# Linear attention before a mixture of experts: scores in four 64x64 tiles, compact states, and their product ahead of the transpositions

## The chip, the core and the metric

The kernel runs on one core of a Trainium2 chip. The metric is the device time of one execution in microseconds, from the median of three runs.

## The reference

Three layers follow each other. The first, the only one that the change touches, is block-wise attention with a decay, over 4 batches, 8 heads, 768 positions and a head size of 64:

```python
for b in range(nb):
    intra = np.einsum('bhic,bhjc->bhij', qb, kb) * Dmask[None]
    intra = np.einsum('bhij,bhjd->bhid', intra, vb)
    inter = np.einsum('bhid,bhde->bhie', qb * lam_pow[None], kv_state)
    out[:, :, sl] = intra + inter
    kb_dec = kb * rev_pow[None]
    kv_state = lam_block[None, :, None, None] * kv_state + np.einsum('bhsd,bhse->bhde', kb_dec, vb)
```

So each block has scores of its own (`intra`) and reads a 64x64 state per head (`inter`), which it then renews. The second layer is a soft mixture of 8 experts with 32 slots over the 3072 tokens, the third a dense layer with a sigmoid-approximated GELU, out of `w_in` (512x2048) and `w_out` (2048x512).

## The kernel before, in words

All is fp32. The attention takes blocks of 128 positions in place of the reference's 64, which is the same sum. Its unit of work is a step: one batch, one half of the sequence (384 positions, three chunks of 128) and one pair of heads. There are 32 steps (`NSTEP`); four of them, the four pairs of heads, make a group, and groups alternate between the first and the second half of a batch. The two heads of a pair stand in partitions 0 to 63 and 64 to 127.

For a step s the functions are, with the lines of the profile:

- `do_q` and `do_T` (L250, L259, L261): ScalarE reorders q, TensorE transposes q and k against an identity, and ScalarE copies both out of their banks as qT (L269) and kT (L272).
- `do_SC` (L297, L300): the score products kT times qT, per chunk one matmul for each head, in rows 0 to 63 or 64 to 127 of the array; VectorE multiplies with the decay and writes AT. The two heads have a bank each, s0 and s1.
- `do_kd` (L285): k times its decay, on ScalarE. `do_qd` (L278): qT times the powers of lambda, on POOL.
- `do_ST` (L310, L319, L321): kd times v, a 64x64 product per head and chunk; VectorE adds it to the decayed state before. A state is a 128x128 tile with the two heads on its diagonal and zeros elsewhere, which POOL writes once (L517). The state of the last chunk of a first half is kept for the second half (`S_3`).
- `do_XS` (L336): the product of the states with qdT, per chunk one matmul over all 128 rows. It opens the bank x. In the first half of a sequence its first chunk has no state and is left out.
- `do_XA` (L344): AT times v is added in the same bank; ScalarE then copies the bank out as xT (L347).
- `do_XT` (L355, L356): xT is transposed back and stored as xn for the mixture of experts.

The eight banks are named and each is single, so a writer waits until the tile before in its bank has been read. The order on each engine is the order in which the loop (L531) calls these functions: an iteration i issues the scores of step i + 1, the transpositions of q and k of step i + 2, the transposition back of step i − 1, the state product of step i, the new states of step i + 1, kd of step i + 2 and AT times v of step i. Between them stand parts of the mixture of experts, spread over four iterations (`ph`): with `ph` 0 the logits of the group before and the slots of the one before that (L365, L437), with `ph` 1 the transposition of the logits (L374), with `ph` 2 a maximum (L408), with `ph` 3 the exponentials (L423, L429, L431).

In every second iteration from 2 to 20 a block of `w_in` or `w_out` is brought to its range by ScalarE, VectorE and POOL in `do_early` (L180, L189 to L195, L202); its transfer, `stage`, was issued on SP an iteration earlier. SP also issues the loads of q, k and v, three to five steps ahead, and those of the expert weights.

Of the kernel before, what the change touches and what calls it, by code (L numbers as in the profile page):

```python
# [8 lines left out]
F32 = mybir.dt.float32  # L9
# [3 lines left out]
ALU = mybir.AluOpType  # L13
# [4 lines left out]
def attention_moe_gelu_kernel(  # L18
# [14 lines left out]
    PE, ACT, DVE, POOL, SP = nc.tensor, nc.scalar, nc.vector, nc.gpsimd, nc.sync  # L33

    B, H, S, D = q.shape
    P = 128
    NHP = H // 2
    HS = 384
    R = HS // P
# [10 lines left out]
    NSTEP = NG * NHP  # L50
# [25 lines left out]
    attn = attn_cm.__enter__()  # L76
# [154 lines left out]
        by_turns(conversion(("early", c), o, POOL))  # L231


    S_a = [attn.tile([P, P], F32, tag=f"sa{i}", name=f"sa{i}", bufs=1) for i in range(4)]
    S_3 = [attn.tile([P, P], F32, tag=f"s3{i}", name=f"s3{i}", bufs=1) for i in range(NHP)]

    def state(s, c):

        b, hf, hp, g = step_of(s)
        if c == R:  # L240
            return S_3[hp]
        return S_a[2 * (s % 2) + (c - 1 if c < R else c - R - 1)]
# [46 lines left out]
    def do_SC(s):  # L289

        b, hf, hp, g = step_of(s)
        bs = [bank(f"s{h}", "bs") for h in range(2)]
        for c in range(R):
            cs = slice(c * P, (c + 1) * P)
            for h in range(2):
                hs = slice(h * D, (h + 1) * D)
                PE.matmul(bs[h][:, cs], kT[s][hs, cs], qT[s][hs, cs], start=True, stop=True)  # L297
        for h in range(2):
            t = attn.tile([P, R, P], F32, tag=f"AT{h}", name="AT")
            DVE.tensor_tensor(out=t, in0=bs[h][:, :HS].rearrange("m (c i) -> m c i", c=R),  # L300
                              in1=dec[:, 2 * hp + h, None, :].to_broadcast([P, R, P]), op=ALU.mult)
            AT[s, h] = t

    def do_ST(s):
        b, hf, hp, g = step_of(s)
        bst = bank("st", "bst")
        nchunk = [c for c in range(R) if hf * R + c < NHF * R - 1]
        for c in nchunk:
            for h in range(2):
                PE.matmul(bst[h * D:(h + 1) * D, c * D:(c + 1) * D], kd[s][:, c, h, :],  # L310
                          v_t[s][:, c, h, :], start=True, stop=True)
        for c in nchunk:
            cg = hf * R + c
            new = state(s, cg + 1)
            for h in range(2):
                r = slice(h * D, (h + 1) * D)
                src = bst[r, c * D:(c + 1) * D]
                if cg == 0:
                    DVE.tensor_copy(out=new[r, r], in_=src)  # L319
                else:  # L320
                    DVE.scalar_tensor_tensor(out=new[r, r], in0=state(s, cg)[r, r],  # L321
                                             scalar=qtab[r, hp, P - 1:P], in1=src,
                                             op0=ALU.mult, op1=ALU.add)

    bxs = {}

    def do_XS(s):

        b, hf, hp, g = step_of(s)
        bx = bxs[s] = bank("x", "bx")  # L330


        first = hf * R
        chunks = [c for c in range(R) if first + c > 0]
        for c in chunks:
            PE.matmul(bx[:, c * P:(c + 1) * P], state(s, first + c), qdT[s][:, c, :],  # L336
                      start=(c == chunks[0]), stop=False)

    def do_XA(s):

# [138 lines left out]
    with tc.manual_schedule():  # L479
# [27 lines left out]
        n = 1  # L507
# [5 lines left out]
        load_step(2, "k")  # L513
        load_step(2, "q")
        load_step(3, "q")
        for t in S_a + S_3:
            POOL.memset(t, 0.0)  # L517
        POOL.memset(ones, 1.0)

        def make_isum():  # L520
# [10 lines left out]
        for i in range(-2, NSTEP):  # L531
            g, ph = divmod(i, NHP)
            if i > -2:
                load_step(i + 5, "q")
            if i == 1:
                make_isum()

            if 0 <= i + 1 < NSTEP:
                do_SC(i + 1)
            if 0 < i + 2 < NHP:  # L540

                for h in range(2):
                    make_dec(2 * (i + 2) + h)

            if 0 <= i + 2 < NSTEP:
                do_T(i + 2)
                if i == -2:
                    warm_up(1)
            if 0 <= i - 1 < NSTEP:
                do_XT(i - 1)  # L550
            if 0 <= i + 3 < NSTEP:
                do_q(i + 3)
            if ph == 1 and 0 <= g - 1 < NG:
                tail_L(g - 1)
            if ph == 2 and 0 <= g - 1 < NG:
                tail_max(g - 1)
            if ph == 3 and 0 <= g - 1 < NG:
                tail_exp(g - 1)
            if i == NSTEP - 1:
                tail_logits_first(NG - 1)  # L560
            if 0 <= i < NSTEP:
                do_XS(i)

            if 0 <= i + 1 < NSTEP:
                do_ST(i + 1)
            if 0 <= i + 2 < NSTEP:
                do_kd(i + 2)
            if 0 <= i < NSTEP:
                do_XA(i)

            if ph == 0 and 0 <= g - 1 < NG:
                tail_logits(g - 1)
            if ph == 0 and 0 <= g - 2 < NG:
                tail_z(g - 2, "tk")
                tail_slot(g - 2)
                tail_acc(g - 2)
            if i == NSTEP - 4:
                load_pieces(i + 1)

            load_pieces(i)  # L580

            load_step(i + 5, "k")
            c, turn = divmod(i - 2, EVERY)
            if turn == 1 and 0 <= c + 1 < len(EARLY):
                load_early(c + 1)
            if i >= 0:
                load_step(i + 3, "v")
            if 0 <= i + 2 < NSTEP:
                do_qd(i + 2)
            if i == -2:  # L590
                load_step(2, "v")
                SP.dma_start(out=phi_sb, in_=phi.rearrange("(k p) s -> p k s", p=P))
            if turn == 0 and 0 <= c < len(EARLY):
                do_early(c)
            if ph == 3 and 0 <= g - 1 < NG and i < NSTEP - 1:
                tail_row(g - 1)
            if ph == 0 and 0 <= g - 2 < NG:
                tail_row_exp(g - 2)
            if i == NSTEP - 2:
                early_cm.__exit__(None, None, None)  # L600
                slotb_cm = tc.tile_pool(name="slotb", bufs=NPC_B, side="right", reuse_waits="tile")
                slotb = slotb_cm.__enter__()

                rooms = [piece_room(NPC + j) for j in reversed(range(NPC_B))]
                while rooms:
                    load_piece(rooms.pop())
            if i == NSTEP - 1:
                attn_cm.__exit__(None, None, None)
                slotc_cm = tc.tile_pool(name="slotc", bufs=NPC_C, side="left", reuse_waits="tile")
                slotc = slotc_cm.__enter__()  # L610
                for _ in range(NPC_C):
                    load_piece()
# [712 lines left out]
```

## Time and profile before

| | |
|---|---|
| Median of three runs | 488.8 us (488.13 to 491.09) |
| Profiled execution | 490.36 us |
| Its span, first to last instruction | 488.5 us |
| TensorE busy (PE) | 471.3 us |
| VectorE (DVE), ScalarE (ACT), POOL | 369.8, 302.6, 77.7 us |
| Attention loop, 6.59 to 147.94 us | 141.35 us; TensorE busy 136.29, VectorE 112.85, ScalarE 102.58 |

PEld is TensorE's weight load, which can run beside a matmul. An fp32 matmul leaves two weight loads and two matmul records in the trace, a transposition one of each. A record lasts longer than its stream, since matmuls are pipelined, so that records overlap; the chain counts them end to end. "Idle before" is the time an engine stood still in front of an instruction, with what released it.

### The profile page before, as it was taken

Reading aid. Unit: us, or ns where it says so; the run is one execution under the profiler, and the core shown is the slowest. Engines: PE = TensorE matmul, PEld = TensorE weight load, DVE = VectorE, ACT = ScalarE, POOL = GpSimd, SP = SyncE. Lnnn points to the kernel's source line nnn. Section 1 sums busy time; section 2 is a strip of 40 time slices with the busy share of each in tenths; the row PEclk is TensorE's granted clock in tenths of the full one; section 3 lists DMA queues with packets and bytes.
Section 4 is the critical chain, followed back from the end, with each engine's and each line's share of the span. In section 5 each row is a group of like instructions: output and inputs, shape, how many; then the busy total and the mean of one; then the engine's idle time right before and its main releaser. Section 6 shows DMA issues by size and latency. Waiting matters only on the chain.

```text
span 488.5 us, 10721 instructions
## 1 busy us (share of the span) xinstructions
PE 471.3 (96%) x4019; PEld 391.2 (80%) x4019; DVE 369.8 (76%) x895; ACT 302.6 (62%) x605; POOL 77.7 (16%) x125
## 2 busy tenths in 40 slices
PE   7999999999999999999999999999999999999992
PEld 4877778878876344878788778888999999999991
DVE  5767788888974112897787689998678888888993
ACT  5777587677754324876865877565665555556540
POOL 3544354352221000000000000000001011101111
PEclk9999999999999999999999999999999999999997
DMA  7999999999999998366633532100401233123334
GB/s 185 285 283 257 275 260 289 274 281 269 245 345 350 363 395 318 91 204 204 230 119 106 209 129 87 43 1 1 155 20 16 29 45 44 16 28 45 46 44 86
DMA packets 85604, 81.52 MB, mean 167 GB/s; under 512 B 54704, under 2 KB 62896, under 8 KB 85552
## 3 DMA queue, kind: packets, MB, share of 16 engines
q1 hardware_dynamic: 83104, 76.63, 50.5%
q0 software_dynamic: 2304, 4.20, 6.4%
q8 instruction: 32, 0.52, 0.5%
q14 instruction: 20, 0.16, 0.1%
q10 hardware_dynamic: 144, 0.00, 0.0%
HBM read 69.80 MB, written 11.01 MB: 165 GB/s over the span
## 4 chain that ended last, share of the span: by engine, by line
PE 81%; DVE 9%; DMA 7%; ACT 2%; issue 1%; POOL 0%; DVEq 0%; ACTq 0%
PE bo L1000 26%; PE bp L1166 22%; PE bs L297 4%; PE bacc L769 3%; DMA stage<-in_moe_w_in_dram 3%; PE bh L747 3%; PE bx L344 3%; PE bx L336 3%; PE bsh L1122 2%; PE bhh L953 2%; PE bq L259 2%; PE bst L310 2%; PE bt L355 2%; DVE AT L300 1%; PE bk L261 1%; PE bp L437 1%
## 5 line engine op out<-in xcount | busy, mean ns | idle before, releaser
L1000 PE MATMUL bo<-wlo,GHI 128*128 128x512 f32 x192 | 75.3, 395 | 0.1
L1000 PE MATMUL bo<-whi,GLO 128*128 128x512 f32 x192 | 75.1, 394 | 0.0
L1000 PE MATMUL bo<-whi,GHI 128*128 128x512 f32 x192 | 74.8, 393 | 0.1
L1136 ACT ACTIVATE GHI<-G_all 128x896 fp32r<-128x896 f32 x48 | 45.8, 954 | 45.8 <-DVE G_all L1129 45.7
L1129 DVE TENSOR_TENSOR G_all<-G_all 128x128 f32<-128x128 f32 x192 | 47.4, 288 | 19.8 <-ACT G_all L1125 17.3
L1196 POOL DMA_DIRECT2D out_dram<-f x16 | 14.3, 1049 | 278.9 <-DVE G_all L1129 272.7
L1166 PE MATMUL bp<-tc,GHI 128*128 128x256 f32 x288 | 55.8, 282 | 0.0
L1141 DVE TENSOR_TENSOR GLO<-G_all,GHI 128x896 fp32r<-128x896 f32 x48 | 52.1, 1084 | 0.0
L961 ACT ACTIVATE G_all<-bhh 128x384 f32<-128x384 f32 x64 | 28.2, 490 | 34.9 <-PE bhh L953 34.7
L1166 PE MATMUL bp<-whi,GHI 128*128 128x256 f32 x192 | 49.5, 281 | 0.0
L1166 PE MATMUL bp<-wlo,GHI 128*128 128x256 f32 x192 | 49.2, 282 | 0.0
L1166 PE MATMUL bp<-whi,GLO 128*128 128x256 f32 x168 | 47.6, 283 | 0.0
L1166 PEld LDWEIGHTS bp<-tc,GHI 128*128 128x128 f32 x288 | 44.4, 190 | 0.0
L1000 PEld LDWEIGHTS bo<-wlo,GHI 128*128 128x128 f32 x192 | 36.0, 188 | 9.6 <-issue 2.5
L1000 PEld LDWEIGHTS bo<-whi,GLO 128*128 128x128 f32 x192 | 36.0, 188 | 7.8 <-DVE GLO L967 0.3
L1000 PEld LDWEIGHTS bo<-whi,GHI 128*128 128x128 f32 x192 | 36.1, 188 | 7.4 <-DVE W2s L907 0.5
L1166 PE MATMUL bp<-tc,GLO 128*128 128x256 f32 x144 | 40.4, 280 | 0.0
L967 DVE TENSOR_TENSOR GLO<-G_all,GHI 128x768 fp32r<-128x768 f32 x32 | 30.6, 955 | 10.4 <-ACT GHI L964 10.2
L278 POOL TENSOR_TENSOR qdT<-qT,qtab 128x384 f32<-128x384 f32 x32 | 32.4, 1012 | 37.9 <-PE bx L336 19.3
L297 PEld LDWEIGHTS bs<-qT,kT 64*128 64x128 f32 x384 | 25.6, 187 | 13.5 <-DVE zsum L457 4.2
L1166 PEld LDWEIGHTS bp<-wlo,GHI 128*128 128x128 f32 x192 | 34.7, 190 | 0.0
L297 PE MATMUL bs<-qT,kT 64*128 64x128 f32 x384 | 32.2, 290 | 2.5 <-DVE AT L300 1.3
(230 smaller groups left out, 1046.7 us busy)
## 6 DMA issues: line engine op xcount, KB each, us to landing
w<-in_moe_w_dram SPq DMA_DIRECT2D x64, 512.0 KB, 6.3
f<-in_moe_w_out_dram SPq DMA_DIRECT2D x15, 512.0 KB, 3.4
qr<-in_q_dram SPq DMA_DIRECT2D x32, 192.0 KB, 4.2
k<-in_k_dram SPq DMA_DIRECT2D x64, 96.0 KB, 4.3
v<-in_v_dram SPq DMA_DIRECT2D x64, 96.0 KB, 4.0
f<-in_moe_w_in_dram SPq DMA_DIRECT2D x12, 512.0 KB, 3.9
out_dram<-o SPq DMA_DIRECT2D x24, 256.0 KB, 2.8
out_dram<-f POOLq DMA_DIRECT2D x16, 256.0 KB, 5.3
```

Source lines behind the costliest of these rows:

```text
L278: POOL.tensor_tensor(out=qdT[s], in0=qT[s].rearrange("m (c i) -> m c i", c=R), in1=qtab[:, hp, None, :].to_broadcast([P, R, P]), op=ALU.mult)
L297: PE.matmul(bs[h][:, cs], kT[s][hs, cs], qT[s][hs, cs], start=True, stop=True)
L336: PE.matmul(bx[:, c * P:(c + 1) * P], state(s, first + c), qdT[s][:, c, :], start=(c == chunks[0]), stop=False)
L344: PE.matmul(bx[h * D:(h + 1) * D, c * P:(c + 1) * P], v_t[s][:, c, h, :], AT[s, h][:, c, :], start=False, stop=(c == R - 1))
L747: PE.matmul(bh[g * NS:(g + 1) * NS, :FQ], sT[:, kk, :], w_pc["w1", e, kk][:, g * FQ:(g + 1) * FQ], start=(kk == 0), stop=(kk == KD - 1), t ...
L961: ACT.activation(out=g[j][:, u * HS:(u + 1) * HS], in_=bh[j][u][:, :HS], func=AF.Gelu_apprx_sigmoid)
L967: DVE.tensor_tensor(out=glo[j][:, o], in0=g[j][:, o], in1=ghi[j][:, o].bitcast(F32), op=ALU.subtract)
L1000: PE.matmul(ob[t], a[j][:, t * P:(t + 1) * P], w[f], start=(begin and i == 0), stop=(end and i == 2))
L1129: DVE.tensor_tensor(out=o, in0=x, in1=y, op=op)
L1136: ACT.activation(out=sh[j], in_=gs(j)[:, P:], func=AF.Copy)
L1141: DVE.tensor_tensor(out=sl[j], in0=gs(j)[:, P:], in1=sh[j].bitcast(F32), op=ALU.subtract)
L1166: PE.matmul(bank_of(gi, i)[1], x, w, start=begin, stop=end)
```

## The change

The scores of a chunk and a head are split by the rows of the output: four matmuls per chunk with 64x64 weights in place of two with 64x128. The states are 128x64 tiles, the two heads one above the other, renewed by one VectorE operation per chunk in place of two; the memsets of the old tiles go. The state product becomes two matmuls per chunk with 64x64 weights, one per head, on the array's diagonal. And `do_XS(i)` is called right behind `do_SC(i + 1)`, in front of the transpositions, where it stood behind them and behind the group's small products.

```diff
-    S_a = [attn.tile([P, P], F32, tag=f"sa{i}", name=f"sa{i}", bufs=1) for i in range(4)]
-    S_3 = [attn.tile([P, P], F32, tag=f"s3{i}", name=f"s3{i}", bufs=1) for i in range(NHP)]
+    S_a = [attn.tile([P, D], F32, tag=f"sa{i}", name=f"sa{i}", bufs=1) for i in range(4)]
+    S_3 = [attn.tile([P, D], F32, tag=f"s3{i}", name=f"s3{i}", bufs=1) for i in range(NHP)]
+    HR = [slice(h * D, (h + 1) * D) for h in range(2)]
...
-            for h in range(2):
-                hs = slice(h * D, (h + 1) * D)
-                PE.matmul(bs[h][:, cs], kT[s][hs, cs], qT[s][hs, cs], start=True, stop=True)
+            for a in range(2):
+                for h in range(2):
+                    PE.matmul(bs[h][HR[a], cs], kT[s][HR[h], c * P + a * D:c * P + (a + 1) * D], qT[s][HR[h], cs],
+                              start=True, stop=True)
...
-            for h in range(2):
-                r = slice(h * D, (h + 1) * D)
-                src = bst[r, c * D:(c + 1) * D]
-                if cg == 0:
-                    DVE.tensor_copy(out=new[r, r], in_=src)
-                else:
-                    DVE.scalar_tensor_tensor(out=new[r, r], in0=state(s, cg)[r, r],
-                                             scalar=qtab[r, hp, P - 1:P], in1=src,
-                                             op0=ALU.mult, op1=ALU.add)
+            src = bst[:, c * D:(c + 1) * D]
+            if cg == 0:
+                DVE.tensor_copy(out=new, in_=src)
+            else:
+                DVE.scalar_tensor_tensor(out=new, in0=state(s, cg), scalar=qtab[:, hp, P - 1:P], in1=src,
+                                         op0=ALU.mult, op1=ALU.add)
...
-        chunks = [c for c in range(R) if first + c > 0]
-        for c in chunks:
-            PE.matmul(bx[:, c * P:(c + 1) * P], state(s, first + c), qdT[s][:, c, :],
-                      start=(c == chunks[0]), stop=False)
+        todo = [(c, h) for c in range(R) if first + c > 0 for h in range(2)]
+        for n, (c, h) in enumerate(todo):
+            PE.matmul(bx[HR[h], c * P:(c + 1) * P], state(s, first + c)[HR[h]], qdT[s][HR[h], c, :],
+                      start=(n < 2), stop=False)
...
-        for t in S_a + S_3:
-            POOL.memset(t, 0.0)
...
                 do_SC(i + 1)
+            if 0 <= i < NSTEP:
+                do_XS(i)
...
-            if 0 <= i < NSTEP:
-                do_XS(i)
```

On TensorE, a step with `ph` 0 in a second half stood so before: scores (bs), transpositions of q (bq) and k (bk), transposition back (bt), three state products (bx from s and sa), new states (bst), AT times v (bx from AT).

```order
L297 MATMUL bs<-qT,kT 128x128 x6
L259 MATMUL bq<-ident,q 128x128 x3
L261 MATMUL bk<-ident,k 128x128 x3
L355 MATMUL bt<-ident,xT 128x128 x3
L336 MATMUL bx<-qdT,s_108 128x128
L336 MATMUL bx<-qdT,sa_104 128x128
L336 MATMUL bx<-qdT,sa_105 128x128
L310 MATMUL bst<-v,kd 64x64 x4
L344 MATMUL bx<-AT,v 64x128 x6
```

The state products stood behind nine transpositions. The same step now, with the semaphores that each instruction waits for:

```order
L298 MATMUL bs<-qT,kT 64x128 [waits DVE_49,Activation_49]
L298 MATMUL bs<-qT,kT 64x128 [waits DVE_49]
L298 MATMUL bs<-qT,kT 64x128 x10
L335 MATMUL bx<-qdT,s_108 64x128 [waits Activation_49,Pool_49]
L335 MATMUL bx<-qdT,s_108 64x128
L335 MATMUL bx<-qdT,sa_104 64x128 [waits DVE_49]
L335 MATMUL bx<-qdT,sa_104 64x128
L335 MATMUL bx<-qdT,sa_105 64x128 [waits DVE_49]
L335 MATMUL bx<-qdT,sa_105 64x128
L260 MATMUL bq<-ident,q 128x128 x3
L262 MATMUL bk<-ident,k 128x128 [waits DMAHW4_49,DMAHW3_49]
```

The six state products have moved in front of the transpositions. Their first waits for ScalarE (Activation_49), which is the copy xT of the step before out of the same bank, and for POOL's qdT; the others wait for VectorE's states. On VectorE, a second-half step with `ph` 1 stood so before (AT, the logits' reductions, then the states):

```order
L300 TENSOR_TENSOR AT<-bs,dec 128x384 x2
L376 TENSOR_REDUCE L<-bL 128x96
L378 TENSOR_REDUCE cm<-L 128x128
L321 SCALAR_TENSOR_TENSOR sa_104<-s_110,qtab,bst 64x64 x2
L321 SCALAR_TENSOR_TENSOR sa_105<-sa_104,qtab,bst 64x64 x2
```

A first-half step now stands so:

```order
L302 TENSOR_TENSOR AT<-bs,dec 128x384 x2
L375 TENSOR_REDUCE L<-bL 128x96
L377 TENSOR_REDUCE cm<-L 128x128
L319 COPY sa_104<-bst 128x64
L321 SCALAR_TENSOR_TENSOR sa_105<-sa_104,qtab,bst 128x64
L321 SCALAR_TENSOR_TENSOR s_110<-sa_105,qtab,bst 128x64
```

Nothing has moved on VectorE; each pair of 64x64 operations is one of 128x64. The orders of ScalarE and SP stay, and POOL's loses its memsets.

## Rows read from the trace of the kernel before

**Rows 1.** The page's first part (busy us, share, instructions) and second (busy tenths in 40 slices)
```profile
PE 471.3 (96%) x4019; PEld 391.2 (80%) x4019; DVE 369.8 (76%) x895; ACT 302.6 (62%) x605; POOL 77.7 (16%) x125
...
DMA  7999999999999998366633532100401233123334
```

**Rows 2.** The chain that ended last, 98.5 to 140.5: start us, us, engine, tile, line, records
```profile
104.85 0.87 PE bs L297 x12
...
107.18 0.67 PE bx L336 x6
...
108.89 0.87 PE bs L297 x12
...
112.71 0.87 PE bs L297 x12
...
116.76 0.87 PE bs L297 x12
...
122.06 0.87 PE bs L297 x12
...
125.99 0.87 PE bs L297 x12
...
128.10 0.45 PE bx L336 x4
...
129.04 0.66 PE bx L344 x12
129.70 0.87 PE bs L297 x12
...
133.41 0.87 PE bs L297 x12
...
138.97 0.87 PE bs L297 x12
```

**Rows 3.** Timeline of one step: start us, us, engine, instruction, idle before and releaser
```profile
126.78 0.31 PEld L259 LDWEIGHTS bq<-ident,q 128*128 128x128 f32 x3
...
127.43 0.72 ACT L269 ACTIVATE qT<-bq 128x384 f32<-128x384 f32 x1 [0.83 <-PE bq L259]
...
129.63 0.94 PE L297 MATMUL bs<-qT,kT 64*128 64x128 f32 x12
...
129.85 0.47 ACT L347 ACTIVATE xT<-bx 128x384 f32<-128x384 f32 x1
```

**Rows 4.** Timeline of the step at 98.89, TensorE and ScalarE
```profile
98.89 1.30 PE L297 MATMUL bs<-qT,kT 64*128 64x128 f32 x12 [0.35 <-DVE AT L300]
...
99.40 0.28 ACT L429 ACTIVATE e<-a 128x96 f32<-128x96 f32 x1 [0.46 <-DVE a L425]
...
99.68 0.79 ACT L285 ACTIVATE kd<-k,dec 128x192 f32<-128x192 f32 x2
...
100.12 0.55 PE L259 MATMUL bq<-ident,q 128*128 128x128 f32 x3
100.37 0.47 ACT L347 ACTIVATE xT<-bx 128x384 f32<-128x384 f32 x1
```

**Rows 5.** The chain, 88 to 99
```profile
92.56 4.21 DMA stage<-in_moe_w_out_dram
...
98.75 0.14 issue
```

**Rows 6.** Groups by line, 20 to 160 us: count, busy us, mean ns, idle before
```profile
L297 PEld LDWEIGHTS bs<-qT,kT 64*128 64x128 f32 x336 | 22.6, 187 | 11.8 <-DVE zsum L457 4.2 <-ACT xn L356 2.8 <-ACT kd L285 2.4
...
L344 PEld LDWEIGHTS bx<-AT,v 128*64 128x64 f32 x355 | 19.9, 137 | 0.1
...
L321 DVE SCALAR_TENSOR_TENSOR sa<-sa,qtab,bst 64x64 f32<-64x64 f32 x58 | 16.3, 280 | 1.9
```

**Rows 7.** Timeline, the logits' matmuls in four 32-column tiles
```profile
103.08 0.85 PE L365 MATMUL bl<-xT,phi_sb 128*32 128x384 f32 x8
```

**Rows 8.** Timeline, POOL's first work after its memsets
```profile
6.92 1.01 POOL L278 TENSOR_TENSOR qdT<-qT,qtab 128x384 f32<-128x384 f32 x1 [4.40 <-DVE qtab L509]
```

## The prediction

> **What bounds the kernel now.** I read the page first: TensorE is busy for 471.3 of 488.5 us [rows 1], so a wait of the others matters only where TensorE ends up waiting too. The change touches the attention loop alone, and there I read the chain that ended last. The loop has 32 steps; a step is what lies from one group of score products (L297) to the next. In the chain the undisturbed steps hold TensorE work only: in that at 125.99 the scores take 0.87 us, the state product (L336) comes at 128.10 and AT times v (L344) at 129.04, and the next scores follow at 129.70 [rows 2]. Steps repeat in fours, because the logits and slots of the MoE are spread over them: 4.04, 3.82, 4.05 and 5.30 us from 104.85 to 122.06, then 3.93, 3.71, 3.71 and 5.56 to 138.97 [rows 2]. The first of a four transposes logits; the fourth, with the slots, is the long one. The state product has three chunks (6 records, 0.67 us) in one four and two (4 records, 0.45) in the next [rows 2]; the long step already has the number of the four that follows.
>
> Then I read ScalarE beside TensorE in one step, on the timeline [rows 3]. The first q transposition loads its weights at 126.78. ScalarE idles 0.83 us until the q transpositions are done and starts qT at 127.43, 0.64 after that load. It then works in its own order without a hole: qT, kT, xn, q, two kd, and last xT, the copy that empties the bank of the state product. xT ends at 129.85 + 0.47 = 130.32: 2.89 us from qT's start, and 0.69 after the next scores began (129.63).
>
> **The change part by part.** *State product in front of the transpositions.* There is one bank x, so the product of step s cannot begin before ScalarE has copied out that of step s − 1. Before, the transpositions stood between the scores and the product: TensorE came to it 128.10 − 125.99 = 2.11 us into the step [rows 2], and a copy that ended at 0.69 was long done. Now TensorE comes to it right behind the scores, at about 0.70. And behind the product wait, in TensorE's order, the transpositions of q and k, which start ScalarE's next round. That closes a loop: xT, state product, q transpositions, qT and on to xT.
>
> Let "rest" be TensorE's time from the first transposition to the next scores without the state product; the change leaves it alone. It is the step less 0.87 and less its product. First steps of a four: 4.04 − 0.87 − 0.67 = 2.50, and 3.93 − 0.87 − 0.45 = 2.61. Second steps: 2.28 and 2.39. Third steps: 2.51 and 2.39. Long ones: 5.30 − 0.87 − 0.45 = 3.98 and 5.56 − 0.87 − 0.67 = 4.02. xT now ends X = 0.64 + 2.89 − rest = 3.53 − rest into the step that follows, however late that round began. After a first step X is 1.03 or 0.92, after a second 1.25 or 1.14. In a third step ScalarE also has e and al, 0.28 us from start to start (99.40 to 99.68 [rows 4]), so X is 1.30 or 1.42 after it. After a long one it is below zero.
>
> The product begins a semaphore's time after X: between 0 and the 0.14 that stands between VectorE's AT and the scores in the chain [rows 5]; I take 0.05. Another 0.05 is its first weight load, now exposed, and 0.09 the change of tiling behind it (the scores' 0.87 less six times 0.11 of stream and a first load of 0.10 leave 0.11). The transpositions so start at X + 0.19 plus the product, where they started at 0.87 before: a step grows by X − 0.68. Second steps: 0.35 and 0.24. Third: 0.57 and 0.46. Long ones: 0.62 and 0.74. First steps wait for nothing and keep the gain of 0.08 that comes below. The two fours from 104.85 to 138.97 cost 1.46 and 1.36, together 2.8.
>
> The four fours before them are disturbed: a transfer of w_in or w_out, which VectorE converts, lands late in the third step, as the 4.21 us piece at 92.56 in the chain [rows 5]. The conversion delays AT and the next scores wait for AT, which stretches the third step already; its growth is hidden there, all but 0.1. But VectorE's lateness also holds ScalarE's e, kd and xT. In the step at 98.89 xT ends at 100.84, 1.95 into it, while the transpositions ran from 100.12, at 1.23 [rows 4]. The product would begin at 2.00 and the transpositions at 2.00 + 0.05 + 0.67 + 0.09 = 2.81; with the product gone from behind them that step grows by 2.81 − 1.23 − 0.67 = 0.91. Where VectorE is less late it is nearer to the 0.62 of above. Such a four costs −0.08 + 0.3 + 0.1 + 0.6 to 0.9, about 1.0; four of them 4.0. The first four steps and the last ones have no long step with slots among them; I take 0.8 for all of these.
>
> *Scores in four tiles.* 12 matmuls in place of 6, 24 records in place of 12, each with 64 columns of weights and 128 streamed. Now two row tiles run side by side. If all four do, the stream stays six times 0.11 us (as the 12 records of AT times v, 0.66 [rows 2]), and only the exposed first load shrinks, by the 50 ns between records of 187 and 137 ns [rows 6]. With 0.01 from the stream that is 0.06 a step; the other end is tiles in pairs only, 12 x 0.11 = 1.32 in place of 0.66. I take four abreast, since the logits with their 32-column tiles do so: 8 records of 384 columns end within 0.85 us [rows 7], and one such record streams for over 0.3 at the rate of AT times v. The Trainium skill (TensorE: Matmul & The Clock Gate, section "Packing small matmuls — row/col tiling") says that a weight load overlaps matmuls in flight only where the row group differs, which two of the four tiles here don't do; by it the dear end would hold. The logits' four tiles share all rows and still run together, so the trace speaks against it.
>
> *State product in two tiles.* 12 or 8 records in place of 6 or 4, in pairs on the diagonal: 6 x 0.11 = 0.66 against 0.67. I take 0.02 of gain; unpaired it would be 0.66 dearer. The number of tiling changes in a step stays three. With the scores' 0.06 that makes the 0.08.
>
> *Compact states.* Three VectorE operations of 128x64 replace six of 64x64 at 280 ns [rows 6]. Their free size is the same, so I take 280 each: 0.84 us of VectorE's time a step goes (nothing, if 128 partitions took twice as long). In undisturbed steps TensorE doesn't wait for VectorE, so I count no gain; but it covers the earlier product, which needs the last state 1.4 us earlier than it did. Without the halving about 0.3 more would be due in second steps.
>
> *No memsets.* POOL's eight at the start lie in the 4.40 us in which its first qdT waits for VectorE's table [rows 8]: nothing. No other order of POOL, ScalarE or SP changes, and no DMA moves past another; the k and stage loads on SP wait for kd, which moves 0.2 to 0.5 later, inside what is taken for the disturbed fours.
>
> **Sum.** 2.8 + 4.0 + 0.8 = 7.6 us more. On the profiled execution, 490.36 us (span 488.5 and 1.9 around it), that makes 498.0. It was 1.6 above the median of the three runs, 488.8, so the median should come to 496.4. About 1% (4.9 us) is what can be told from no change.
>
> **Rivals.** *Landings hold the loop* (slower, but within 1%). If the stage transfers land when they do now, whatever TensorE does, each disturbed four gives its 1.0 back in its third step, and so do the first steps. 7.6 − 4.0 − 0.8 = 2.8 is left: 491.6. For it: the DMA engines are taken for 90% or more of all slices there [rows 1]. Against it: SP issues these transfers behind k loads that wait for ScalarE's kd, so they move with the loop.
>
> *Pairs, not fours.* The scores take 0.05 + 1.32, and the product comes at 1.37, when xT is mostly out: a step grows by 1.37 + 0.09 − 0.87 = 0.59, in 32 steps 19, of which four third steps hide 0.5 each: 17 us, 505.8. Against it stand the logits' rows [rows 7]; no row has 64x64 tiles. This is what the rule of the Trainium skill named above (TensorE: Matmul & The Clock Gate) would do here.
>
> *VectorE was the bound* (the other side). At 98.89 the scores wait for AT and take 1.30 in place of 0.87 [rows 4]. If 0.84 us less work a step lets VectorE be on time, six such steps give 0.4 each and TensorE its 32 x 0.08 = 2.6: 5.0 less, 483.8. It decides only from the point at which xT is out within 0.65 of a step, so if ScalarE's round from qT took 2.29 us in second steps in place of 2.89. For it: AT is what the chain shows in front of those scores. Against it: VectorE is late there because of a landing.
>
> **How the numbers follow.** Forecast 0.62 (491.5 to 501), landings 0.17, pairs 0.08, VectorE 0.13. The range from 485.0 to 503.5 leaves out the pairs and most of the VectorE case. Slower by over 1% (above 493.7): nine tenths of the forecast and the pairs, 0.64. Faster (below 483.9): half of the VectorE case and a little for the unforeseen, 0.09. Within 1%: the rest, 0.27.
>
> **What would show it.** Right: in second, third and long steps TensorE stands idle for 0.2 to 0.8 us in front of the state product, released by xT; steps of 3.71 become about 3.95 (second) and 4.17 (third), and 5.56 becomes 6.3; ScalarE still idles in front of qT; score records come in fours 0.11 us apart; VectorE is busy some 22 us less (80 operations of 280 ns). Wrong: products that start right behind the scores; scores that stream over 1.2 us; waits there that end with VectorE's states.

## The result, and the profile after

The changed kernel takes 497.1 us (median of four runs, 496.4 to 498.1) against 489.9 for the kernel before on the same chip (488.1 to 491.5): a ratio of 1.0145, 95% interval 1.0118 to 1.0172, 7.1 us more. The profiled execution took 496.43 us (span 494.6) where before took 490.36, 6.1 more.

The page of the kernel after, first part and transfers, against [rows 1]:

```profile
PE 470.6 (95%) x4563; PEld 384.1 (78%) x4563; DVE 349.7 (71%) x815; ACT 299.6 (61%) x605; POOL 75.7 (15%) x117
...
DMA  7999999998889999247644542100310233123334
```

VectorE lost 80 instructions and 20.1 us, as the change intends, and TensorE's busy time hardly moved: the change saved the time of an engine that did not set the end. The loop's transfers fall from 9s to 8s in places, since the loop got longer, not its loads larger.

The timeline of the kernel after, the scores of nine steps in a row (start us, us, engine, line, instruction):

```profile
107.33 0.89 PE L298 MATMUL bs<-qT,kT 64*64 64x128 f32 x24
...
111.31 1.01 PE L298 MATMUL bs<-qT,kT 64*64 64x128 f32 x24
...
115.68 0.89 PE L298 MATMUL bs<-qT,kT 64*64 64x128 f32 x24
...
120.28 0.89 PE L298 MATMUL bs<-qT,kT 64*64 64x128 f32 x24
...
126.29 0.89 PE L298 MATMUL bs<-qT,kT 64*64 64x128 f32 x24
...
130.15 0.89 PE L298 MATMUL bs<-qT,kT 64*64 64x128 f32 x24
...
134.14 0.89 PE L298 MATMUL bs<-qT,kT 64*64 64x128 f32 x24
...
138.25 0.89 PE L298 MATMUL bs<-qT,kT 64*64 64x128 f32 x24
...
144.51 0.89 PE L298 MATMUL bs<-qT,kT 64*64 64x128 f32 x24
```

Subtract neighbours. The two fours of [rows 2], 4.04, 3.82, 4.05, 5.30 and 3.93, 3.71, 3.71, 5.56, are now 3.98, 4.37, 4.60, 6.01 and 3.86, 3.99, 4.11, 6.26. First steps gained 0.07, all others lost.

The step at 130.15, ScalarE and TensorE, against [rows 3]:

```profile
130.57 0.48 ACT L346 ACTIVATE xT<-bx 128x384 f32<-128x384 f32 x1
...
131.13 0.44 PEld L335 LDWEIGHTS bx<-qdT,sa 64*64 64x64 f32 x8 [0.33 <-issue]
...
131.75 0.55 PE L260 MATMUL bq<-ident,q 128*128 128x128 f32 x3
...
132.39 0.69 ACT L270 ACTIVATE qT<-bq 128x384 f32<-128x384 f32 x1 [1.33 <-PE bq L260]
```

xT is out at 131.05, 0.90 into the step. TensorE has had nothing to do for 0.33 us and loads the states' product at 131.13; the q transpositions follow at 131.75, 1.60 into the step, and ScalarE, which starts its next round with qT, has idled 1.33 us (0.83 before). Each waits for the other once a step. So it stands in the view of waits of the kernel after, 6 to 155 us (waiter, what it waited for: us in total, times, longest):

```profile
ACT qT L270 <- PE bq L260: 36.8, 27, 1.9
...
DVE stage L189 <- DMA stage<-in_moe_w_in_dram: 7.0, 4, 2.4
...
PEld bx L335 <- issue: 8.2, 15, 0.9
...
PEld bx L335 <- POOL ra L464: 5.3, 6, 0.9
...
PE bx L335 <- ACT xT L346: 4.7, 9, 0.7
...
ACT w_in L180 <- DMA stage<-in_moe_w_in_dram: 4.3, 5, 2.0
```

In the same view of the kernel before, ScalarE's wait in front of qT is 12.2 us, the one for w_in's landing 13.1:

```profile
ACT w_in L180 <- DMA stage<-in_moe_w_in_dram: 13.1, 8, 2.9
ACT qT L269 <- PE bq L259: 12.2, 18, 1.0
```

POOL's qdT, for which the product waits too, does not hold it: in the step at 130.15 the product reads a qdT that ended at 124.72, 6.4 us before. The row above that names POOL is one to distrust. In the step at 120.28:

```profile
120.91 0.34 POOL L464 TENSOR_TENSOR ra<-L,rm 128x96 f32<-128x96 f32 x1 [0.64 <-ACT kd L286]
121.14 0.48 ACT L346 ACTIVATE xT<-bx 128x384 f32<-128x384 f32 x1
...
121.69 0.44 PEld L335 LDWEIGHTS bx<-qdT,sa 64*64 64x64 f32 x8 [0.76 <-POOL ra L464]
```

POOL was done at 121.25; the product starts 0.07 after xT's end at 121.62. It is the same wait for the bank.

### The profile page after: what moved, and what is told of

It reads as the page before. It is cut to its first block, busy times and chain, and to the rows that moved or that the text cites. A ratio compares the mean times of both kernels' runs of the same rounds, so it can differ in the third digit from the quotient of the medians.

```text
span 494.6 us, 11658 instructions
## 1 busy us (share of the span) xinstructions
PE 470.6 (95%) x4563; PEld 384.1 (78%) x4563; DVE 349.7 (71%) x815; ACT 299.6 (61%) x605; POOL 75.7 (15%) x117
## 4 chain that ended last, share of the span: by engine, by line
PE 65%; issue 10%; DMA 9%; DVE 8%; ACT 5%; SPq 2%; POOL 1%; DVEq 0%; ACTq 0%; POOLq 0%
PE bo L996 25%; PE bp L1162 12%; PE bacc L765 3%; PE bh L743 3%; DMA stage<-in_moe_w_in_dram 3%; PE bx L335 3%; DMA out_dram<-f 2%; PE bhh L949 2%; PE bx L343 2%; DMA w<-in_moe_w_dram 2%; PE bq L260 2%; PE bs L298 2%; PE bsh L1118 1%; ACT kd L286 1%; POOL out_dram L1192 1%
## 5 line engine op out<-in xcount | busy, mean ns | idle before, releaser
L270 ACT ACTIVATE qT<-bq 128x384 f32<-128x384 f32 x32 | 22.4, 699 | 38.9 <-PE bq L260 36.8
L302 DVE TENSOR_TENSOR AT<-bs,dec 128x384 f32<-128x384 f32 x64 | 32.4, 547 | 5.8 <-PE bs L298 5.6
```

Of the source, the lines that this page charges most:

```text
L270: ACT.activation(out=t.rearrange("m (p c) -> m c p", c=R), in_=bq[:, :HS].rearrange("m (c p) -> m c p", c=R), func=AF.Copy)
```

## The experiments

One measure serves for all of them: the **stretch** from the scores of step 1 to those of step 31, 30 steps of the loop, read from the timeline. Ratios are to the kernel before on the same chip; fours are the sums of steps 2 to 5, 6 to 9 and so on, the last being 26 to 29. A stretch comes from one profiled execution of each kernel, and the times of one kernel differ by 1 to 7 us from execution to execution, so a difference of stretches of 1 or 2 us is a hint, unless single steps or the medians bear it out.

| kernel | median us | ratio, 95% interval | stretch us | its seven fours |
|---|---|---|---|---|
| before | 489.9 | | 133.81 | 17.26 19.10 19.46 18.02 18.05 17.21 16.91 |
| after | 497.1 | 1.0145 [1.0118, 1.0172] | 139.38 | 19.09 19.09 18.72 19.12 18.85 18.95 18.23 |
| before, product in front | 499.6 | 1.0196 [1.0163, 1.0229] | 138.69 | 17.77 18.57 18.95 19.22 19.43 19.21 18.09 |
| before, four score tiles | 491.6 | 1.0030 [1.0014, 1.0046] | 135.31 | 17.92 18.76 18.27 19.61 18.88 17.21 16.57 |
| after, product behind | 490.9 | 1.0024 [1.0003, 1.0046] | 132.76 | 16.24 18.13 19.07 18.21 17.76 18.32 17.57 |
| after, xT first | 494.9 | 1.0095 [1.0061, 1.0129] | 137.71 | 19.57 18.69 18.30 19.01 18.76 17.96 18.26 |
| before, 8 pieces late | 496.1 | 1.0107 [1.0063, 1.0151] | 133.00 | 16.78 18.28 19.08 18.07 18.02 17.47 16.76 |
| after, 8 pieces late | 503.1 | 1.0258 [1.0223, 1.0292] | 138.29 | 17.67 19.54 18.44 18.93 18.66 18.93 18.24 |
| score tiles, 8 late | 497.2 | 1.0124 [1.0081, 1.0167] | 133.59 | 16.46 17.94 18.65 18.17 18.72 18.49 16.56 |
| product behind, 8 late | 497.4 | 1.0141 [1.0105, 1.0177] | 132.10 | 19.27 18.32 17.37 17.52 17.65 17.46 17.02 |
| after, two banks | 495.0 | 1.0123 [1.0077, 1.0170] | 136.27 | 16.75 20.33 19.78 18.33 18.05 18.14 17.05 |
| after, guard on VectorE | 499.5 | 1.0204 [1.0146, 1.0261] | 141.78 | 17.66 20.13 21.98 18.93 18.75 18.91 18.24 |
| before, no conversions | 485.8 | 0.9887 [0.9807, 0.9967] | 126.97 | 16.73 17.21 17.11 17.21 16.76 17.44 16.76 |
| after, no conversions | 494.6 | 1.0089 [1.0057, 1.0121] | 136.43 | 17.66 18.74 18.23 18.82 18.24 18.81 18.23 |

### Which part of the change costs

The product back behind the transpositions, all else as changed:

```diff
             if 0 <= i + 1 < NSTEP:
                 do_SC(i + 1)
-            if 0 <= i < NSTEP:
-                do_XS(i)
...
+            if 0 <= i < NSTEP:
+                do_XS(i)
             if 0 <= i + 1 < NSTEP:
                 do_ST(i + 1)
```

> The changed kernel with the state product back behind the transpositions; the four score tiles, the compact states and the product in two 64x64 tiles stay. If the wait for xT in front of the early product is the cost (the loop theory), that wait is gone: TensorE comes to the product 2 us into a step, xT is out by 0.7. What is left is a fourth change of tiling in a step, some 0.14 us with its exposed weight load, against 0.08 of gain: plus 0 to 2.5 us on the kernel before, steps of 3.71 at about 3.75. If the 64x64 tiles themselves are the cost (rival), it stays 5 to 8 us slower than before.

490.9 us, ratio 1.0024: with these two lines moved back, a loss of 1.45% becomes one of 0.24%. In the view of waits of this kernel, 6 to 154 us, ScalarE's wait in front of qT is short again, and no row has the product waiting for xT:

```profile
ACT qT L270 <- PE bq L260: 13.6, 17, 1.3
```

The reverse, in the kernel before only the product moved in front (the + lines above are its - lines):

> The kernel before with the one edit that its state product, still 128x128 over zero-padded states, is called right behind the scores. The loop theory: the same waits for xT as in the changed kernel, without the 0.08 us a step of gain and without VectorE's relief: 8 to 11 us slower than before. The rival, that the shape of the tiles and not the place costs: within 2 us of the kernel before.

499.6 us, 1.0196: the move alone makes the kernel slower, more than the whole change does. Its view of waits, 6 to 154 us:

```profile
ACT qT L269 <- PE bq L259: 38.4, 30, 2.3
...
PE bx L336 <- ACT xT L347: 6.6, 14, 0.8
```

Its stretch is 4.9 us longer. Another 3.3 us of its profiled execution lie behind the scores of step 31; 1.5 of them are one wait of TensorE for ScalarE's copy of the output, which itself waits 2.9 us for an output transfer; the kernel before has no such wait there. Why it comes up here is not shown.

In the kernel before only the scores in four tiles:

```diff
-            for h in range(2):
-                hs = slice(h * D, (h + 1) * D)
-                PE.matmul(bs[h][:, cs], kT[s][hs, cs], qT[s][hs, cs], start=True, stop=True)
+            for a in range(2):
+                for h in range(2):
+                    hs = slice(h * D, (h + 1) * D)
+                    PE.matmul(bs[h][a * D:(a + 1) * D, cs], kT[s][hs, c * P + a * D:c * P + (a + 1) * D], qT[s][hs, cs],
+                              start=True, stop=True)
```

> The kernel before with only the scores in four 64x64 tiles. Four abreast: 0.06 us less in each of 32 steps, 1.9 us less in all, scores of 0.81 us in the chain in place of 0.87. Tiles in pairs only (rival): scores of 1.4 us and 17 to 20 us more.

The step's gain is there, the total's is not: the last four falls from 16.91 to 16.57 us, but the stretch grows by 1.5 and the total by 0.3%. The view of waits of this kernel, 6 to 155 us, has waits for v that were 0.4 and 0.8 us before:

```profile
PEld bst L312 <- DMA v<-in_v_dram: 3.4, 3, 1.4
...
PE bst L312 <- DMA v<-in_v_dram: 2.9, 3, 1.2
```

By difference of stretches the parts are: four score tiles +1.5 us; compact states and their product in two tiles −2.6 (132.76 − 135.31); the move in front +6.6 (139.38 − 132.76); together +5.6. The move by itself, in the kernel before, gave +4.9. The medians bear out the move (1.0145 against 1.0024) and the loss of the score tiles (1.0030, interval above 1); for the compact states they show nothing clear (490.9 against 491.6 us).

### Is it the order on ScalarE?

If the wait for xT is the cost, xT ahead of kd on ScalarE should end it:

```diff
             if 0 <= i + 1 < NSTEP:
                 do_ST(i + 1)
+            if 0 <= i < NSTEP:
+                do_XA(i)
             if 0 <= i + 2 < NSTEP:
                 do_kd(i + 2)
-            if 0 <= i < NSTEP:
-                do_XA(i)
```

> The changed kernel with ScalarE's two kd behind xT in place of in front of it. The loop theory: xT then ends about 0.55 us into the next step in place of 0.9 to 1.4, under the 0.70 at which the scores are through, so the idle time in front of the state product goes and the long steps fall from 6.3 to about 5.5; the kernel comes out at 1 to 4 us less than before. The rival (tiles or VectorE's states hold the product) keeps it 5 us or more above the kernel before.

494.9 us: 2 us better than the change, 4.7 worse than before, where 1 to 4 better was expected. The idle time in front of the product went: it starts 0.60 to 0.77 us into 25 of 31 steps, and steps of 3.58 to 3.68 us appear, as short as the shortest of before (3.60). But kd now stands behind ScalarE's in-order waits, and the new states wait for kd. In the timeline of this kernel:

```profile
25.98 0.75 PE L312 MATMUL bst<-v,kd 128*64 128x64 f32 x7 [2.37 <-ACT w_in L180]
```

ScalarE stood at the conversion of w_in, whose landing was late, with kd behind it, and that one step took 6.60 us. Right behind this wait TensorE's granted clock was 0.50 from 26.97 to 30.39 us, which adds about 1.2 us to the next step (an estimate, worked out in the last section). The wait was moved, not removed.

### Do landings hold the loop?

DMA engines are taken for 90% or more of the loop, so I thought that TensorE's gains were given back at landings. Here the loop asks for less:

```diff
-            n = min(NPC, max(0, i + 1) * NPC // (NSTEP - 1), NPC - 1 if i < NSTEP - 5 else NPC)
+            n = max(0, i + 1) * (NPC - 8) // (NSTEP - 1) if i < NSTEP - 2 else NPC
```

> The kernel before; only the loads of the expert weights are paced otherwise: 24 of their 32 pieces (512 KB each) go out over the loop and the last 8 together ahead of the last two steps, so the loop asks for 4.2 MB less, some 15.6 us of transfers at the 268 to 286 GB/s of the loop. Theory (landings): the loop of before stands at the limit of its transfers (share 0.98 to 0.99), ScalarE's and VectorE's 24.9 us of waits for the stage fall below 8 us, the disturbed fours shorten to the 17 us of the undisturbed ones, and the loop ends 3 to 5 us sooner than at 147.9 us; the total falls by less, or not, since the experts wait for the 8 pieces. Rival (engines): the waits for the stage cost TensorE nothing, the loop ends at 147.4 to 148.4 us and the total is the same or longer.

> The changed kernel with the same pacing of the weight pieces. Theory (landings): its loop (153.5 us) was held less by landings (waits of 11.3 us for the stage) and gains only 0.5 to 2.5 us; against the kernel before with the same pacing the loop is 7 to 9 us longer where it was 5.5, which is what the wait behind the transpositions costs in all eight fours, as in the sum of 7.6 us. Rival (engines): the difference stays at 5.5 us.

> The kernel before with the four score tiles alone and the same pacing. Theory (landings): freed of the landings the gain of 0.05 us per step shows, and the loop ends 1.2 to 2 us sooner than that of the kernel before with this pacing; the waits of TensorE for v (6.3 us) fall below 2. Rival: the four tiles lose elsewhere, and the loop ends at the same time or later, as it did (149.3 against 147.9 us).

> The changed kernel with the states' product back behind the transpositions, and the same pacing. Theory (landings): scores (1.6 us) and the shorter product (about 0.3 to 0.6 us) show, the loop ends 1.5 to 2.5 us sooner than that of the kernel before with this pacing. Rival: compact states bring nothing beside the scores, the loop ends as with the four score tiles alone or later.

That theory fell. The loop of before became 0.8 us shorter, not 3 to 5; the difference between after and before stayed at 5.3; the score tiles lost 0.6 instead of gaining 1.2 or more. The product behind came 0.9 below before, short of the 1.5 expected; but in its first four, 19.27 us, TensorE's granted clock was 0.50 from 27.22 to 30.63 us, worth up to 2.0 (an estimate, in the last section), so without that it would probably have passed the mark. The totals rose by 5 to 7 us, since the experts now wait for the pieces. The view of waits of before with 8 pieces late, 150 to 260 us, where the kernel before has 1.9 us in its first row:

```profile
PEld bacc L769 <- DMA w<-in_moe_w_dram: 6.7, 8, 1.3
...
PEld bh L747 <- DMA w<-in_moe_w_dram: 2.6, 5, 1.1
```

### Is it the single bank?

Two banks for the product in turns; the sums for the states move into free columns of the banks of q and k:

```diff
-        bx = bxs[s] = bank("x", "bx")
+        bx = bxs[s] = bank(("x", "st")[s % 2], "bx")
...
-        bst = bank("st", "bst")
+        bq, bk = bqk.pop(s + 1) if s + 1 < NSTEP else (bank("tq", "bst"), bank("tk", "bst"))
+        bst = [bq[:, HS:HS + D], bq[:, HS + D:HS + 2 * D], bk[:, HS:HS + D]]
```

> The changed kernel with two banks for the attention sums x, taken in turns by even and odd steps; the second is that of the states' sums, which move into the free columns of the banks of the transposed q and k. Theory (single bank): the states' product no longer waits for ScalarE's copy of the sums of the step before; it starts within 0.1 us of the end of the scores unless VectorE's states come later, undisturbed steps fall back from 3.87 to 4.1 us to 3.65 to 3.8, the stretch from the scores of step 1 to those of step 31 falls from 139.4 us to 132.5 to 135 (133.8 before), and the total is 489 to 492 us. Rival (place): what counts is that the transpositions and with them ScalarE's round start 0.65 us later; then the stretch stays above 137 us and the total above 494.

In the last four the answer is plain: 17.05 us against 18.23. The product follows the scores at once (timeline of the kernel with two banks):

```profile
129.64 0.89 PE L300 MATMUL bs<-qT,kT 64*64 64x128 f32 x24
130.35 0.62 PE L338 MATMUL bx<-qdT,sa 64*64 64x128 f32 x8
```

In the four before it the third and the long step fall from 4.60 and 6.01 us to 4.10 and 5.57 (4.05 and 5.30 in the kernel before). So the bank is the cause in undisturbed third and long steps. The second steps gain little or nothing: 4.50 and 3.89 against 4.37 and 3.99, where before took 3.82 and 3.71. The stretch, 136.27 us, lies between the two theories, and the total is 495.0, where one expected at most 492 and the other more than 494. Two things are left. In front of the transpositions the product also needs VectorE's states 1.4 us sooner, and after a late AT they are not there (same kernel, step at 111.57):

```profile
112.94 0.28 DVE L324 SCALAR_TENSOR_TENSOR sa<-sa,qtab,bq 128x64 f32<-128x64 f32 x1
112.96 0.51 PEld L338 LDWEIGHTS bx<-qdT,sa 64*64 64x64 f32 x8 [0.42 <-DVE sa L324]
```

And there are two steps of 5.27 and 5.74 us in the second and third four, in which the new states came 4.2 to 4.4 us into the step; the second of them waited 1.45 us for v. Whether the moved sums had a part in these two is open. They do bring a wait of their own, for ScalarE's copy qT out of the bank of q:

```profile
PE bq L315 <- ACT qT L272: 5.8, 15, 1.2
```

That is from the view of waits, 6 to 155 us, and the second step at 129.64 has one of these. So this kernel shows the second bank at less than its worth.

### Is it VectorE beside POOL?

In the kernel after, at 71.7 us, a tiny operation of VectorE lasts as long as POOL's beside it:

```profile
71.69 0.73 POOL L203 TENSOR_TENSOR w_in<-stage,w_in 128x256 f32<-128x256 f32 x1 [0.43 <-DVE stage L195]
71.75 0.71 DVE L473 TENSOR_SCALAR rs<-rs 128x3 f32<-128x3 f32 x1
```

I took this for the reason why VectorE is late in second steps, and gave POOL's part of the ten early conversions to VectorE:

```diff
-        by_turns(conversion(("early", c), o, POOL))
+        by_turns(conversion(("early", c), o, DVE))
```

> The changed kernel with the last operation of the ten early conversions on VectorE (one of 128x256) in place of two on POOL. Theory (shared port): VectorE's 128x3 sums of the second steps, 0.71 to 0.75 us beside POOL's operation, take 0.16 to 0.2 us; the second steps of rows 11, 15, 19 and 23 fall from 4.4 to 4.6 us to 4.1 to 4.3, and the total by 0.5 to 2 us against the changed kernel (497.1). Rival: the small sums stay long or VectorE is late for another reason, the second steps stay at 4.4 us or more and the total within 0.5 us of 497.1 or above.

The collision at this operation ended, in all four places where it stood, and nothing came of it. The same operation four microseconds later in that kernel's run, with the one that VectorE took over ahead of it:

```profile
75.51 0.42 DVE L199 SCALAR_TENSOR_TENSOR w_in<-w_in,stage 128x256 f32<-128x256 f32 x1
...
76.13 0.17 DVE L473 TENSOR_SCALAR rs<-rs 128x3 f32<-128x3 f32 x1
```

Second steps of 4.66, 4.34, 4.51 and 4.35 us stand against 4.45, 4.54, 4.58 and 4.37: no change. Two steps of 5.23 and 8.21 us came in: behind a late landing the operation that VectorE took over lasts 1.06 us beside POOL's qdT (0.42 where it stands alone), and AT starts 4.54 us into the step. In the step of 8.21 us TensorE's granted clock was 0.50 from 66.98 to 70.39 us, worth about 1.5 of it (an estimate, in the last section). The total is 2.4 us above the change. The port shows in the durations. Whether it makes the second steps long this run cannot tell: the edit takes 0.54 us off VectorE's sum and puts 0.42 us more work right in front of it.

### What covered the wait?

What the disturbed fours have and the last one has not are the ten early conversions. Both kernels without them:

```diff
     def load_early(c):
-        src, r, o, dst = EARLY[c]
-        SP.dma_start(out=stage[:, :2 * CB], in_=src[r:r + P, 2 * o:2 * (o + CB)])
-        staged["early", c] = stage[:, :2 * CB].rearrange("p (n t) -> p n t", t=2)
+        pass
...
-        convert_abs(("early", c), o)
-        by_turns(conversion(("early", c), o, POOL))
+        POOL.memset(o, 0.0)
```

> The kernel before without the ten early conversions (the first of the later weights stay zero: their loads into the stage, ScalarE's absolute values, VectorE's three and POOL's two operations on each are left out, POOL writes zeros in their place). Theory (cover): the conversions and the landings that they wait for are what lengthens the disturbed fours; all seven fours from row 2 on take the 16.9 us of rows 26 to 29, and the stretch from the scores of step 1 to those of step 31 falls from 133.8 us to 125.5 to 128 (4.0 + 7 x 16.9 + 4.0 = 126.3). Rival (the rest of the loop): fours of 17.5 us and more remain, and the stretch is above 129.5 us.

> The changed kernel without the ten early conversions, left out in the same way. Theory (cover): every four takes the 18.2 us of rows 26 to 29, the stretch is 134.5 to 136.5 us (3.9 + 7 x 18.23 + 4.0 = 135.5), and stands 8 to 10 us above that of the kernel before without them, where with them it stood 5.6 above: the conversions of the kernel before hid some 3 to 4 us of the wait for the bank. Rival: both stretches fall alike, and the difference stays at 5 to 6.5 us.

The scores of steps 1 and 31 in the timeline of before without conversions:

```profile
9.54 0.94 PE L294 MATMUL bs<-qT,kT 64*128 64x128 f32 x12 [0.29 <-ACT kT L269]
...
136.51 0.94 PE L294 MATMUL bs<-qT,kT 64*128 64x128 f32 x12
```

and of after without conversions, with one four in between:

```profile
9.34 0.89 PE L295 MATMUL bs<-qT,kT 64*64 64x128 f32 x24 [0.29 <-ACT kT L270]
...
49.50 0.89 PE L295 MATMUL bs<-qT,kT 64*64 64x128 f32 x24
...
53.37 0.89 PE L295 MATMUL bs<-qT,kT 64*64 64x128 f32 x24
...
57.35 0.89 PE L295 MATMUL bs<-qT,kT 64*64 64x128 f32 x24
...
61.46 0.89 PE L295 MATMUL bs<-qT,kT 64*64 64x128 f32 x24
...
67.72 0.89 PE L295 MATMUL bs<-qT,kT 64*64 64x128 f32 x24
...
145.77 0.89 PE L295 MATMUL bs<-qT,kT 64*64 64x128 f32 x24
```

126.97 and 136.43 us: 9.5 apart, where with the conversions it is 5.6. Both came within what the theory of the cover said. The four from 49.50, steps of 3.87, 3.98, 4.11 and 6.26, now repeats the last one. The conversions cost the kernel before 6.8 us of stretch and the changed one 3.0: the 3.9 between them is what they hid of the wait. Less traffic alone had not done that (the runs with 8 pieces late took 4.2 MB out of the loop, these 2.6), so it is something in the conversions themselves that covers: their work on ScalarE, VectorE and POOL, their place in the engines' orders or their waits for the stage. These runs took all three out together and do not part them.

## Why the prediction was right

The forecast of 496.4 met 497.1, and its mechanism is what the runs show: the product in front waits for the one bank, and with it ScalarE's next round. But the sum was closer than its terms, and that is luck: errors of several terms cancelled (measured, term by term as below: 3.1 + 1.15 + 1.45 − 0.1 + 0.5 = 6.1). The base moved as well: 496.4 was 488.8 + 7.6, and 497.1 is 489.9 + 7.1; the 6.1 is the difference of the two profiled executions.

- **Undisturbed fours**, 2.8 forecast: 1.74 and 1.32, together 3.1. Step by step (forecast, then measured): second 0.35 and 0.24, then 0.56 and 0.28; third 0.57 and 0.46, then 0.55 and 0.40; long 0.62 and 0.74, then 0.70 and 0.70; first −0.08, then −0.07. X = 3.53 − rest held in each of the six: forecast 1.03, 0.92 (second steps), 1.25, 1.14 (third), 1.30, 1.42 (long), measured 1.02, 0.90, 1.23, 1.11, 1.34, 1.44. In the step at 130.15 the transpositions start at 1.60, forecast 0.92 + 0.19 + 0.45 = 1.56; the parts of the 0.19 (semaphore, first load, change of tiling) had no row each, but their sum came out at 0.23 to 0.27 in the five of these steps in which VectorE's states were in time. The 0.56 was the second of a four behind a conversion, where VectorE's states came later than xT.
- **Disturbed fours**, 4.0 forecast: −0.01, −0.74, 1.10 and 0.80, together 1.15. This is the step that failed. The text had it that the third step's growth "is hidden there, all but 0.1", so +0.4 for four of them. They became 1.8 us shorter (19.21 to 17.41 in sum), and w_in's landing is waited for 4.3 us in place of 13.1: the conversions are no longer late in them. A slower loop is enough for that, and so is VectorE's relief: the same four steps are 16.99 us with only the product in front, where VectorE's work is that of before, and 16.52 with the product behind, where the loop is not slower. Long steps grew by 1.57 and not by 2.4 to 3.6. Second steps went the other way, 1.93 for 1.2: the halved work on the states was counted on to cover the product's need of them 1.4 us sooner, and behind a conversion it did not (in the second step of the third four xT is out at 0.90 us and the last state at 1.95). Without the conversions every four costs 0.9 to 1.6, on average 1.4, as the undisturbed ones.
- **The rest**, 0.8 forecast: 1.45 in steps 1 to 5, and 0.5 outside the stretch. This and the fours missed in opposite directions.
- **Score tiles**: four abreast, 0.05 to 0.06 a step: so it is in six of the eight undisturbed steps of the kernel with the tiles alone; one second step is 0.15 longer and one long step 0.19 shorter. As a term of the total it came to nothing: alone, the tiles made the stretch 1.5 us longer, and 0.6 with fewer transfers. Why, the waits for v tell only in part; it stays open.
- **Product in two tiles**: 0.02 gain forecast. Behind the transpositions, with 8 pieces late, the last four is 17.02 with compact states and 16.56 without: 0.1 a step dearer, not cheaper. With all pieces in the loop it is 17.57 against 16.57, but the long step there holds a wait of 0.45 us for v.
- **Compact states**: no gain forecast, −2.6 us of stretch measured in one pair of kernels and −1.5 in the pair with 8 pieces late (there with up to 2.0 us of halved clock in it), although with that dearer product. The third steps of the disturbed fours, whose scores wait for VectorE's AT [rows 4], fall most: from 20.45 us with the score tiles alone to 16.52. That it is the halved work on the states is argued: no run has the states without the product in two tiles, and the medians show no clear gain.

Of the rivals, *landings hold the loop* was right in its observation (third steps gave back 1.8 us) and wrong in its reason, as the runs with fewer transfers show. *VectorE was the bound* had a point in the disturbed third steps, up to 2.6 us of stretch, and had no chance beside a move that costs 6.6. *Pairs* did not happen: 24 records in 0.89 us.

## What to carry to other kernels

Before moving a product forward in an engine's order, ask who must have emptied its bank, and what waits behind it: here a wait of a few tenths delayed the transpositions that feed the very engine that empties the bank, once in each step. Measure a periodic loop in its cleanest period, but don't multiply that by the number of periods: a stretch that is late for another reason covers part of a new wait, and taking that reason away uncovers it. And time saved on an engine is worth what the late places show, not its busy time: 20 us of VectorE gave 2.6 of stretch at most, and no clear gain in the total.

## What was not expected of the hardware

VectorE's smallest operations, from SBUF to SBUF, stretch to the end of a POOL operation that runs beside them: 0.71 us in place of 0.17 for 128x3 (rows above). In the kernel before, one of 128x1 took 0.99 beside POOL's qdT of 1.00. The Trainium skill (SBUF — State Buffer, section "Who interferes with whom") tells of a port that the two share, and these rows agree; ending the collision at one operation brought no time in the run with the guard on VectorE, which put other work in its place.

Every profiled execution begins with a slower TensorE, and in five of them (product behind, also with 8 late; xT first; two banks; guard on VectorE) this lasts to about 9 us. The first transpositions and a warm-up matmul in the kernel with the product behind:

```profile
5.00 0.87 PE L260 MATMUL bq<-ident,q 128*128 128x128 f32 x3 [0.66 <-ACT q L251]
...
6.31 0.63 PE L488 MATMUL bwarm<-const-bfloat16-1.0 128*128 128x512 bf16 x1
```

and in the kernel after, whose program is the same up to there:

```profile
5.00 0.52 PE L260 MATMUL bq<-ident,q 128*128 128x128 f32 x3 [0.90 <-ACT q L251]
...
5.68 0.38 PE L488 MATMUL bwarm<-const-bfloat16-1.0 128*128 128x512 bf16 x1
```

The view shows the granted clock as 1.00 in both, but the traces' first record of it, at the full 2.4 GHz, comes at 9.28 us in the first kernel and at 3.71 in the second; the view shows 1.00 where there is no record. In the five it comes at 8.7 to 10.2 us, in the other nine at 3.7 to 6.4. In both kernels TensorE had run the same eight warm-up matmuls in the first 4.4 us, which start 0.43 us apart. The scores of step 1 start at 10.4 to 10.7 us in the five and at 8.9 to 9.5 elsewhere, so these executions hold about 1.4 us more at the start; the stretch begins behind it. With one profiled execution of each kernel it is open whether this belongs to the kernel or to the execution.

Inside the loop the granted clock fell in three of these five, to 0.50, the level of 1.2 GHz. The rows of these stretches (guard on VectorE; xT first; product behind with 8 late):

```profile
66.98:70.39 3.41, 3.10 (x20) 2.80 (x21) 0.53 (x2) 0.80 (x2) 0.00 (x0) 0.50 0.73 198
```

```profile
26.97:30.39 3.42, 3.42 (x45) 2.87 (x41) 2.21 (x6) 1.79 (x5) 1.69 (x2) 0.50 0.81 246
```

```profile
27.22:30.63 3.41, 3.41 (x31) 2.90 (x31) 1.40 (x4) 1.83 (x5) 0.89 (x1) 0.50 0.90 254
```

Ahead of the fall TensorE had stood still: 1.27 us for AT and then for xT (guard), 2.37 us in front of the new states' product, for kd (xT first), and 1.20 us in front of the same product (8 late). What it cost I estimate from the same work one step earlier. With 8 late the scores and nine transpositions took 3.92 us and 1.95 the step before, so 2.0 at most, since the scores there wait for AT as well. With xT first the scores and the product took 2.78 after 1.31, and with the guard the product and the transpositions 3.38 after 1.63; less 0.22 for the third chunk of these products, that is 1.2 and 1.5.

No version made here beats the kernel before with the whole computation in it; the product behind comes nearest, and its 0.24% may be that start, if its other executions began like the profiled one.
